# Decode attention beside a gated feed-forward block: key and value tiles of two heads interleaved over partitions, keys transposed as 32-bit pairs

## The chip, the cores and the metric

The kernel runs on one core of a Trainium2 chip. The time is that of the device in microseconds; a kernel is run several times, and only runs in the fast state are compared, by a ratio to runs of the kernel before in the same rounds. A run more than 1.5% above the fastest of its kernel counts as slow; the text says where that was so. A difference is called settled at 2% only where the whole 95% interval of the ratio lies beyond 2%. A profile is one execution. Engines are named as the profile does: PE is TensorE (PEld its weight loads), DVE is VectorE, ACT is ScalarE, SP issues the loads. Each engine has its own list of instructions, its queue. Semaphores tie the lists together.

## The reference

Only the attention part matters here. Four sequences decode one token each. There are 32 query heads over 8 key/value heads, of width 128, and the last 4096 positions of the cache are used:

```python
q = (x @ wq)                                   # 4 x 32 heads x 128
k = k_cache[:, :, Sk - 4096:, :]               # 4 x 8 heads x 4096 x 128, bf16: 33.5 MB
v = v_cache[:, :, Sk - 4096:, :]               # the same again
p = softmax(q @ k.T * 128 ** -0.5)
a = (p @ v) @ wo                               # wq, wo: 4.2 MB each
b = relu(x @ W_gate) * (x @ W_up) @ W_down     # 1.8 MB each
out = g * a + (1 - g) * b                      # g: a sigmoid gate per sequence
```

In all 81 MB are read, and next to nothing is written. Each key is used by four queries only, so the work per byte is small, but keys arrive with the position on the partitions, and both kernels transpose them on the chip so that the score product can contract over the head width.

## The kernel before

32 heads are handled in 8 sets of four. A key tile is one head: 128 partitions with 32 positions each, so that a partition reads one run of 8 KB.

```python
# loads, all from SP
e.dma_start(Ksb[:, slot, :], A_k_cache[bb, kvh, SK-WIN:SK, :].rearrange("(p c) d -> p (c d)", p=128))

def _act_copies_kt(g, i):                      # which key evictions ScalarE makes
    j = g % 4
    return (j, i) in ((2, 1), (2, 3), (3, 1), (3, 3))

# TensorE's order (cut): KT key transposes, PV value product, PT probability transposes, SC scores
for s in range(NSET + 2):
    for j in range(4):
        g = 4 * s + j
        for i in range(4): order.append(("KT", g, i))
        if s >= 2 and j == 1: order.append(("PV", s - 2, 0, 16))
        if s >= 2 and j == 2: order.append(("PV", s - 2, 16, 32))
    for i in range(4): order.append(("PT", s - 1, i))
    for i in range(8): order.append(("SC", s, i))
```

A fill is one PSUM bank. KT fills a bank with eight 128x128 bf16 transposes, and DVE or ACT copies ("evicts") it to SBUF; there are four such banks, so a fill waits for the eviction of the fill four before it. SC makes scores of 4 heads in four column groups of PE; DVE evicts them and takes the maximum; ACT makes the exponentials in four pieces of 1024 columns. PV is made of 128 small matmuls per set, in four column groups. The weights wo come last of all loads.

## Time and profile before

| | before |
|---|---|
| time | 210.8 us (210.76 to 210.85) |
| span of the profile | 209.4 us |
| load stream | about 419 GB/s, no gap |
| time from one set's exponentials to the next's, sets 2 to 7 | 19.0 us |
| last load lands (landing records of the trace) | 201.1 us |

These lines of the page are the busy time and share of each engine, the mean busy share of the 16 DMA engines in 40 slices of the span (9 is 90% or more), what they moved, and the load queue's packets, megabytes and share of 16 engines' span.

```profile
PE 146.9 (70%) x3007; PEld 119.3 (57%) x3007; DVE 128.4 (61%) x338; ACT 86.4 (41%) x116; POOL 0.7 (0%) x6
...
DMA  4999999999999999999999999999999999999710
GB/s 131 415 424 426 412 403 436 412 423 418 423 421 413 419 419 419 423 419 421 423 416 412 423 415 419 419 426 419 415 415 418 421 423 421 415 419 419 299 42 1
...
q1 hardware_dynamic: 12136, 81.02, 93.7%
```

The DMA row is full from slice 2 to 37. The kernel is bound by its loads, and every engine has slack on average.

### The profile page before, as it was taken

The numbers are of one execution on the slowest core, as the hardware profiler recorded it, in microseconds if no ns is written. First come the engines' busy times: TensorE is split into PE (matmuls) and PEld (weight loads), VectorE is DVE, ScalarE is ACT, GpSimd is POOL, SyncE is SP. The second block draws the span as 40 slices with busy tenths as digits, with TensorE's granted clock in tenths as the row PEclk, the third lists the DMA queues.
The fourth block names the chain that finished last, engine by engine and source line by source line (L and its number), as shares of the span: only waits on it lengthen the run. The fifth ranks groups of instructions, "written<-read, shape, count | busy, mean of one in ns | idle before, by whom it ended". The sixth has DMA issues, their size and how long they took to land.

```text
span 209.4 us, 6715 instructions
## 1 busy us (share of the span) xinstructions
PE 146.9 (70%) x3007; PEld 119.3 (57%) x3007; DVE 128.4 (61%) x338; ACT 86.4 (41%) x116; POOL 0.7 (0%) x6
## 2 busy tenths in 40 slices
PE   0029917659997869797797777876976797756362
PEld 0028915459993758486396736753873677345251
DVE  4002914952459927994996499769948975942121
ACT  2000123280271836195466428551754565193000
POOL 1000000000000000000000000000000000000000
PEclk9999988968599997999969999999999999985555
DMA  4999999999999999999999999999999999999710
GB/s 131 415 424 426 412 403 436 412 423 418 423 421 413 419 419 419 423 419 421 423 416 412 423 415 419 419 426 419 415 415 418 421 423 421 415 419 419 299 42 1
DMA packets 12164, 81.43 MB, mean 389 GB/s; under 512 B 1764, under 2 KB 1768, under 8 KB 2792
## 3 DMA queue, kind: packets, MB, share of 16 engines
q1 hardware_dynamic: 12136, 81.02, 93.7%
q8 instruction: 23, 0.38, 0.7%
q14 instruction: 5, 0.04, 0.0%
HBM read 81.01 MB, written 0.00 MB: 387 GB/s over the span
## 4 chain that ended last, share of the span: by engine, by line
PE 44%; DMA 19%; DVE 16%; SPq 10%; issue 9%; DVEq 0%
PE bank L556 23%; DVE sc L765 11%; DMA Ksb<-in_A_k_cache_dram 10%; DMA Vsb<-in_A_v_cache_dram 9%; PE bank L625 8%; SPq L462 7%; PE bank L594 5%; PE bank L524 3%; PE bank L654 2%; DVE X L800 2%; DVE Ksb L752 2%; PE bank L582 2%; SPq L449 1%; SPq L445 1%; SPq L451 1%
## 5 line engine op out<-in xcount | busy, mean ns | idle before, releaser
L556 PE MATMUL bank<-ident,Ksb 128*128 128x128 bf16 x1024 | 74.5, 236 | 17.1 <-DMA Ksb<-in_A_k_cache_dram 9.2
L556 PEld LDWEIGHTS bank<-ident,Ksb 128*128 128x128 bf16 x1024 | 66.6, 107 | 23.6 <-DMA Ksb<-in_A_k_cache_dram 9.7
L752 DVE COPY Ksb<-bank 128x1024 bf16<-128x1024 bf16 x96 | 61.0, 684 | 30.9 <-PE bank L556 30.7
L872 ACT ACTIVATE Ksb<-bank 128x1024 bf16<-128x1024 bf16 x32 | 31.6, 1022 | 47.2 <-PE bank L556 47.2
L881 ACT ACTIVATE sc<-sc,negmax 128x1024 bf16<-128x1024 bf16 x32 | 36.3, 1137 | 33.3 <-DVE negmax L776 33.3
L765 DVE TENSOR_SCALAR_CACHE_REDUCE sc<-bank 128x512 bf16<-128x512 f32 x64 | 39.8, 687 | 2.4 <-PE bank L582 1.7
L582 PE MATMUL bank<-Ksb,qT 128*4 128x512 bf16 x256 | 22.5, 378 | 11.5 <-DVE sc L765 9.7
L625 PE MATMUL bank<-Vsb,pT 128*4 128x128 bf16 x1024 | 19.2, 230 | 10.2 <-issue 8.2
L625 PEld LDWEIGHTS bank<-Vsb,pT 128*4 128x4 bf16 x1024 | 15.8, 89 | 12.6 <-issue 11.2
L582 PEld LDWEIGHTS bank<-Ksb,qT 128*4 128x4 bf16 x256 | 5.4, 81 | 27.0 <-DVE sc L765 22.7
L594 PE MATMUL bank<-ident,sc 128*128 128x128 bf16 x256 | 17.2, 225 | 2.2 <-ACT sc L881 2.1
L594 PEld LDWEIGHTS bank<-ident,sc 128*128 128x128 bf16 x256 | 15.5, 101 | 3.1 <-ACT sc L881 3.0
L872 ACT ACTIVATE pT<-bank 128x1024 bf16<-128x1024 bf16 x16 | 15.6, 1026 | 0.3 <-PE bank L594 0.2
L752 DVE COPY pT<-bank 128x1024 bf16<-128x1024 bf16 x16 | 11.0, 690 | 6.5 <-PE bank L594 6.5
L800 DVE COPY X<-bank 32x16 bf16<-32x16 bf16 x32 | 6.0, 186 | 9.0 <-PE bank L635 8.7
L497 PE MATMUL bank<-xT,Wbig 128*128 128x4 bf16 x128 | 3.6, 166 | 11.1 <-DMA Wbig<-in_A_wq_dram 11.1
L497 PEld LDWEIGHTS bank<-xT,Wbig 128*128 128x128 bf16 x128 | 3.5, 104 | 11.2 <-DMA Wbig<-in_A_wq_dram 11.2
L706 DVE CAST qT<-bank 128x128 bf16<-128x128 f32 x1 | 0.3, 292 | 14.5 <-PE bank L497 14.5
L855 ACT ACTIVATE gsb<-bank 1x4 f32<-1x4 f32 x1 | 0.2, 163 | 16.9 <-PE bank L505 16.9
L524 PE MATMUL bank<-xT,Vsb 128*128 128x4 bf16 x112 | 6.8, 199 | 0.0
L524 PEld LDWEIGHTS bank<-xT,Vsb 128*128 128x128 bf16 x112 | 6.8, 161 | 0.0
L881 ACT ACTIVATION_READ_ACCUMULATOR sc<-sc,negmax 128x1 f32 x32 | 6.0, 186 | 0.0
(44 smaller groups left out, 36.6 us busy)
## 6 DMA issues: line engine op xcount, KB each, us to landing
Ksb<-in_A_k_cache_dram SPq DMA_DIRECT2D x32, 1024.0 KB, 18.7
Vsb<-in_A_v_cache_dram SPq DMA_DIRECT2D x32, 1024.0 KB, 19.0
Wbig<-in_A_wq_dram SPq DMA_DIRECT2D x4, 1024.0 KB, 8.4
Wbig<-in_A_wo_dram SPq DMA_DIRECT2D x4, 1024.0 KB, 22.8
Vsb<-in_B_W_gate_dram SPq DMA_DIRECT2D x1, 1792.0 KB, 22.4
Vsb<-in_B_W_up_dram SPq DMA_DIRECT2D x1, 1792.0 KB, 24.8
Vsb<-in_B_W_down_dram SPq DMA_DIRECT2D x1, 1792.0 KB, 21.4
out_dram<-out SPq DMA_DIRECT2D x4, 1.0 KB
```

The lines of the kernel that those rows point to most:

```text
L462: E.op(lambda bb=bb, kvh=kvh, slot=slot: e.dma_start(Ksb[:, slot, :], A_k_cache[bb, kvh, SK - WIN:SK, :].rearrange("(p c) d -> p (c d)", p ...
L497: E.op(lambda H=H, tt=tt: t.matmul(qb[:, Q_COL + H * 4:Q_COL + (H + 1) * 4], Wbig[:, tt, H * 128:(H + 1) * 128], xT[:, tt * 4:(tt + 1) * 4 ...
L524: E.op(lambda W=W, col0=col0, i=i, tt=tt: t.matmul(gub[:, col0:col0 + 4], W[:, tt, i:i + NFT * 127 + 1:NFT], xT[:, tt * 4:(tt + 1) * 4], s ...
L556: E.op(lambda bk=bk, cc=cc, ch=ch, k3=k3: t.transpose(bankbf[bk][:, cc * 128:(cc + 1) * 128], k3[:, ch, :], ident[:, :]), produces=[(f"trf ...
L582: E.op(lambda bk=bk, j=j, lhsT=lhsT, rhs=rhs: t.matmul(banks[bk][32 * j:32 * j + 4, 0:512], lhsT, rhs, start=True, stop=True, tile_positio ...
L594: E.op(lambda bk=bk, cc=cc, ch=ch, par=par: t.transpose(bankbf[bk][:, cc * 128:(cc + 1) * 128], sc[:, par, ch * 128:(ch + 1) * 128], ident ...
L625: E.op(lambda ob=ob, j=j, par=par, ch=ch, v3=v3: t.matmul(ob[32 * j:32 * j + 4, 0:128], pT[:, par, ch * 128 + 32 * j: ch * 128 + 32 * j + ...
L752: E.op(lambda dst=dst, bk=bk: v.tensor_copy(dst, bankbf[bk][:, :]), produces=[copy_ctr(key)], waits=w)
L765: E.op(lambda par=par, i=i, bk=bk: v.tensor_scalar(sc[:, par, i * 512:(i + 1) * 512], banks[bk][:, :], 1.0, None, op0=ALU.mult, op1=ALU.ma ...
L800: E.op(lambda dst=dst, srcv=srcv: v.tensor_copy(dst, srcv), produces=[("dtrc", copy_event(key))] if q == 3 else [], waits=[("TRF",) + key] ...
L872: E.op(lambda dst=dst, bk=bk: a.activation(dst, bankbf[bk][:, :], ACTF.Copy), produces=[copy_ctr(key)], waits=w)
L881: E.op(lambda par=par, piece=piece: a.activation(sc[:, par, piece * n:(piece + 1) * n], sc[:, par, piece * n:(piece + 1) * n], ACTF.Exp, b ...
```

## The change

It is a rewrite with these parts. A tile is two heads, with even partitions for one and odd for the other, so that a partition reads 16 KB. Two neighbouring bf16 elements are transposed as one 32-bit word, so that half as many transposes are needed; even and odd elements of the head then lie side by side, and the score product is made in two passes over every second element, with a query matrix that has zeros where the other position's words lie. wo is loaded early, and half of its product is made before the end; the last value tile comes in quarters; many small steps at the end are gone. Its intent is faster loads and a shorter tail.

```diff
-                    Ksb[:, slot, :], A_k_cache[bb, kvh, SK - WIN:SK, :].rearrange("(p c) d -> p (c d)", p=128)),
+                     A_k_cache[b, h:h + 2, SK - WIN:SK, :].rearrange("h (r c) d -> r h (c d)", r=64), waits=w)
...
-    return (j, i) in ((2, 1), (2, 3), (3, 1), (3, 3))
+    return f in ((3, 7) if i % 2 == 0 else (1, 4, 7))
...
+    for s in range(2, NSET):
+        o += [("KT", 2 * s), ("PT", s - 1), ("PV", s - 2), ("RS", s - 2), ("KT", 2 * s + 1), ("OQ", s - 2), ("SC", s), ("SW", s)]
+        if s == 6:
+            o.append(("WO", 0))
...
+                        rhs = kt2((2 * s + pair) % KSLOTS)[:, 8 * f:8 * f + 8, jp:128:2, e]
+                        mm(bk[32 * j:32 * j + 8, :], qblk[:, g, 8 * e:8 * e + 8], rhs, e == 0, e == 1, ...)
...
+            mm(banks[OB][32 * pair:32 * pair + 8, 0:128], pT[:, s % 2, c0:c0 + 8],
+               Vsb[:, (2 * s + pair) % VSLOTS, 128 * ch:128 * ch + 128], ch == 0, ch == 63, pos=(0, 32 * pair))
...
+                E.op(lambda r=r, n=n: a.activation(pev[r, :, n], sc[r, :], ACTF.Exp, ...)   # pev: every second element
```

(All cuts are marked with "..."; the rest of the diff replaces helpers, the small projections and the end.) KT now has two tiles of eight fills per set; RS, SW and OQ are small matmuls for the sums, the maximum and the output layout.

## The prediction

> **What bounds the kernel now.** The load stream. In the page's 40 slices the DMA row is 9 from slice 2 to slice 37 and moves about 419 GB/s; section 3 gives the load queue 93.7% of 16 engines' span. Every compute engine has slack: PE is 70% busy, DVE 61%, ACT 41%. The period of a set of four heads is 19.9 us (timeline, score matmuls at 100.8 and 120.6 us), which is its 8.4 MB at 420 GB/s. SP's own waits show that loads are issued far ahead (19 us from issue to landing), so short compute stalls do not reach the stream. The last data land at about 197.7 us, and 11.7 us of tail follow: two output transposes with slow strided copies (0.8 us per set), 128 small WO matmuls at half clock (3.7 us), combine, transpose, four stores. Only the stream and this tail are on the critical path.
>
> **Stream.** Packet records: a 3584 B packet takes 142 ns, 8192 B 312 ns (mean 315), 14336 B 540 ns. That is a line of 0.037 ns per byte plus about 8 ns. The skill's "DMA: Bandwidth & Descriptors", section "Why small descriptors are slow", has a fixed cost per packet of the same kind. Estimate for 16 KB: 616 to 622 ns, against 2 x 315. K and V (67 MB) save 2 to 3.7 us, the gate and up loads (3.5 KB runs become 14 KB) 0.6, wq 0.3; WO (4 KB runs) and the quartered last V lose 0.2. The 512 two-byte packets of gate_w, which now do not precede the large loads, save about 0.4. Sum: 3 to 4.5 us. The last byte lands at about 193.7 us.
>
> **Tail.** WO is loaded early, and half of its product is done before the end. After the last quarter of V: 16 PV matmuls (1 to 1.7 us), normalise 0.5, 16 tiny selection matmuls and a copy 1.5, 8 WO matmuls of 512 columns (1.7 warm, 3.4 at half clock, plus 0.3 latency), one combine 0.7, one store and end 2.7. Estimate 9.3 us in place of 11.7. Gain about 2.4.
>
> **Off the path.** Score columns per set and number of score matmuls are unchanged, but the evictions fall from 8 to 4 per set (0.69 us each); K copies stay at 128 (0.68 DVE, 1.02 ACT); PT copies halve; DVE falls to about 12.5 us per set. PV packs two column groups instead of four: from 2 to about 4 us per set. K transposes fall from 1024 bf16 to 512 of 32 bits. If each costs what a bf16 one does (60 ns), PE needs some 12 us per set; at 270 ns it needs 25, and the kernel becomes PE-bound. "TensorE: Matmul & The Clock Gate", Terms, says that transpose mode is four times faster for FP32; no run here shows it yet. I expect 60 to 130 ns.
>
> **Prediction.** Span 203 us, measured time 204.4 us (the measured time lies 1.4 over the span); 8 in 10: 201 to 209. Faster by over 2%: 0.72; within 2%: 0.19; slower: 0.09.
>
> **What would show it.** DMA slices at 425 to 428 GB/s; 16 KB packets of 616 to 622 ns; last V landing near 193.7; 9 to 9.5 us from there to the end; SP never the cause of a DMA gap; K transposes under 130 ns apiece; PE at half clock or better in the tail.
>
> **What would make it wrong.** 32-bit transposes slow enough (over about 190 ns) that PE paces each set; alternating between two heads 4 MB apart slowing HBM reads, so that 16 KB packets take 640 ns or more; the 8-byte-strided score operand streaming at half rate; PE instruction stalls or a cold clock in the tail; or a longer start, as K0 goes ahead of wq.

## More of the kernel before

The timeline of the kernel before, PE alone (start, duration, engine, line, operation, output<-inputs, shapes, count, and in brackets the idle time before it with what ended it), through one set:

```profile
104.80 5.67 PE L556 MATMUL bank<-ident,Ksb 128*128 128x128 bf16 x64
110.40 1.06 PE L625 MATMUL bank<-Vsb,pT 128*4 128x128 bf16 x64
111.40 1.96 PE L556 MATMUL bank<-ident,Ksb 128*128 128x128 bf16 x32
...
118.72 2.00 PE L594 MATMUL bank<-ident,sc 128*128 128x128 bf16 x32
```

PE goes from keys to values to keys without waiting for ACT, and comes to the probability transposes (118.72) long after the exponentials that they need.

The end of the timeline: the value product of the last set begins when the last values land, the product with wo (which lands until 201.1) follows, then the store:

```profile
191.43 3.58 PE L625 MATMUL bank<-Vsb,pT 128*4 128x128 bf16 x127 [1.94 <-DMA Vsb<-in_A_v_cache_dram]
...
201.45 3.35 PE L654 MATMUL bank<-oq,Wbig 128*128 128x4 bf16 x120 [0.41 <-DVE oq L732]
...
206.81 1.30 SPq L472 DMA_DIRECT2D out_dram<-out  x4
```

```profile
106.61 1.15 ACT L881 ACTIVATE sc<-sc,negmax 128x1024 bf16<-128x1024 bf16 x1 [4.69 <-DVE negmax L776]
...
110.02 1.13 ACT L881 ACTIVATE sc<-sc,negmax 128x1024 bf16<-128x1024 bf16 x1
...
112.50 1.94 ACT L872 ACTIVATE Ksb<-bank 128x1024 bf16<-128x1024 bf16 x2 [1.26 <-PE bank L556]
```

The fourth exponential ends at 111.2 us, and ACT's next duty, a key eviction, does not begin before 112.50 and had to wait for PE. Nobody waits for the exponentials.

## The result

| | before | changed |
|---|---|---|
| time, median | 210.8 us | 238.5 us (237.54 to 239.63) |
| ratio of the fast runs | | 1.131, 95% interval 1.128 to 1.135 |
| span of the profile | 209.4 us | 237.9 us |
| PE busy, 100 to 160 us of the span | 47.6 us | 47.2 us |
| last load lands | 201.1 us | 211.1 us |

A ratio here is the mean time of one kernel's fast runs over that of the other's of the same rounds, so it is not quite the ratio of the medians. The change is 13% slower; a gain of 3% had been predicted.

The same lines of the page, changed kernel, with the row of the granted PE clock (in tenths of full speed):

```profile
PE 176.6 (74%) x2346; PEld 127.7 (54%) x2346; DVE 109.5 (46%) x249; ACT 86.2 (36%) x78; POOL 2.9 (1%) x15
...
PEclk9995967979998599979985999799959999999599
DMA  5999999999999999999999959995899990630000
GB/s 220 414 427 420 437 425 429 427 438 422 393 418 433 435 419 422 435 430 419 424 424 426 419 220 391 435 416 191 372 435 430 422 424 22 222 134 3 0 3 1
...
q1 hardware_dynamic: 6816, 81.01, 81.4%
```

The packets are little more than half as many, and while the stream runs it does run at 425 GB/s. But from the middle on it has holes, and after slice 33 it breaks down. The compute side hands back buffers too late: in the timeline below SP issues the next key load at 141.41 us, just after the last scores that read the buffer (141.36), and slice 24 (136.8 to 142.7 us) moves 220 GB/s. This happens although no engine is near full: PE is at 74% against 70%, and DVE is at 46% against 61% and ACT at 36% against 41%.

When the first exponential of each set starts (timelines of ACT) shows where the time goes:

| set | 0 | 1 | 2 | 3 | 4 | 5 | 6 | 7 | end of span |
|---|---|---|---|---|---|---|---|---|---|
| before, us | 41.8 | 68.4 | 88.7 | 106.6 | 126.5 | 145.5 | 164.5 | 183.7 | 209.4 |
| changed, us | 42.6 | 71.0 | 95.1 | 118.8 | 143.0 | 166.6 | 190.8 | 212.8 | 237.9 |
| later by | 0.8 | 2.5 | 6.4 | 12.2 | 16.5 | 21.1 | 26.3 | 29.2 | 28.5 |

The start and the time after the last exponentials (25.7 and 25.1 us) are nearly equal. The loss arises in the sets, mostly 4 to 6 us in each. From set 2 to set 6 a set takes 23.9 us (95.7 over 4), while the stream needs 19.7 for its 8.4 MB (estimate: 8.4 MB at 425 GB/s).

The timeline of the changed kernel through one such set, exponentials to exponentials, ACT, PE and one load issue of SP (SPq):

```profile
118.82 2.62 ACT L689 ACTIVATE pe<-sc,negmax 64x2048 bf16<-64x2048 bf16 x1 [5.63 <-DVE negmax L602]
...
121.51 2.56 ACT L689 ACTIVATE pe<-sc,negmax 64x2048 bf16<-64x2048 bf16 x1
...
124.14 1.02 ACT L666 ACTIVATE Ksb<-bank 128x1024 bf16<-128x1024 bf16 x1
...
125.22 1.11 PE L328 MATMUL bank<-identf,Ksb 128*128 128x128 f32 x4 [3.69 <-ACT Ksb L666]
...
126.12 1.06 PE L324 MATMUL bank<-sel,pe 128*128 128x32 bf16 x32
...
127.11 5.30 PE L324 MATMUL bank<-Vsb,pT 128*8 128x128 bf16 x128
...
132.55 3.74 PE L328 MATMUL bank<-identf,Ksb 128*128 128x128 f32 x32
...
136.32 1.02 ACT L666 ACTIVATE Ksb<-bank 128x1024 bf16<-128x1024 bf16 x1 [0.31 <-PE bank L328]
...
137.49 3.87 PE L324 MATMUL bank<-Ksb,qblk 128*8 128x512 bf16 x32 [0.95 <-ACT Ksb L666]
...
141.41 0.54 SPq L250 DMA_DIRECT2D Ksb<-in_A_k_cache_dram  x1
...
142.96 2.63 ACT L689 ACTIVATE pe<-sc,negmax 64x2048 bf16<-64x2048 bf16 x1 [5.61 <-DVE negmax L602]
```

This is a loop with no slack in it. The exponentials take until 124.1. Behind them *in ACT's queue* is one key eviction (124.14). PE stands still for 3.69 us before its last key fill, because the bank it needs is that eviction's. Behind the fill *in PE's queue* are the probability transposes (126.12), the value product (127.11, 5.3 us), and the second key tile (132.55). ACT evicts its last fill (136.32); the scores wait 0.95 us for that and take 3.87; the maximum follows, and then the next exponentials. PE works for some 18 us of the 24 and waits in order for the rest. In the kernel before, neither queue had such an obstacle.

The costliest groups of the changed kernel that lie on this loop (line, engine, operation, names, shapes, count | busy us, mean ns of one | idle time just before them and what ended most of it):

```profile
L328 PE MATMUL bank<-identf,Ksb 128*128 128x128 f32 x512 | 68.0, 292 | 36.2 <-ACT Ksb L666 22.1
...
L689 ACT ACTIVATE pe<-sc,negmax 64x2048 bf16<-64x2048 bf16 x16 | 41.5, 2592 | 46.8 <-DVE negmax L602 46.6
L324 PE MATMUL bank<-Vsb,pT 128*8 128x128 bf16 x1024 | 44.3, 253 | 0.6 <-DVE recip L612 0.6
...
L324 PE MATMUL bank<-Ksb,qblk 128*8 128x512 bf16 x256 | 31.6, 624 | 6.9 <-ACT Ksb L666 6.9
```

The mean duration of a pipelined matmul is not its rate. The rates come from the timeline: a 32-bit transpose 117 ns (32 in 3.74 us), a value matmul 41 ns in this set (128 in 5.30 us), and 29 ns where the clock was full (128 in 3.74 us, at 198.6 us).

The stretches around that stand-still (from : to, length, busy time of each engine, then granted PE clock, DMA share, GB/s):

```profile
core 0: us, PE busy (x) PEld busy (x) DVE busy (x) ACT busy (x) POOL busy (x), PEclk, DMA share, GB/s
...
121.60:125.20 3.60, 0.00 (x0) 0.00 (x0) 1.01 (x2) 3.54 (x3) 0.00 (x0) 0.78 1.01 432
125.20:127.10 1.90, 1.88 (x36) 1.80 (x36) 0.31 (x1) 0.73 (x1) 0.00 (x0) 0.50 1.03 440
...
131.00:132.50 1.50, 1.50 (x54) 1.39 (x46) 0.00 (x0) 0.00 (x0) 0.00 (x0) 1.00 0.90 371
```

While PE idles from 121.6 to 125.2 its granted clock falls. It is 0.50 during the probability transposes and half of the value product, and full again by 131. The Trainium skill, "TensorE: Matmul & The Clock Gate", Part 1, describes this: after an idle window of about 3.4 us the clock is halved until PE has been busy for about as long. The trace agrees in kind: the profile counts six such waits of up to 3.7 us, and the records of the clock show a stretch of 3.4 or 6.8 us at 0.5 that begins within 1.7 us of the end of each of the six, before it in four and after it in two. How short a wait can be and still have this effect is a question to which experiments 1 and 11 return. So the wait is paid for twice (experiment 9 tests this).

The end of the changed kernel (timeline): the last exponential, the value product of the last set's first tile, the last eight matmuls of the output projection, and the combine.

```profile
215.50 2.56 ACT L689 ACTIVATE pe<-sc,negmax 64x2048 bf16<-64x2048 bf16 x1
...
220.21 6.47 PE L324 MATMUL bank<-Vsb,pT 128*8 128x128 bf16 x64 [0.56 <-DVE recip L612]
...
233.53 1.89 PE L324 MATMUL bank<-Wbig,oq 128*4 128x512 bf16 x8 [0.32 <-DVE oq L636]
235.46 0.74 DVE L652 SCALAR_TENSOR_TENSOR osum<-bank,gg,t 4x512 bf16<-4x512 f32 x1 [1.98 <-PE bank L324]
```

The end does not follow the last byte either: from 211.1, where that lands, it is still 26.8 us. The end is the chain behind the last scores.

### The profile page after: what moved, and what is told of

Same layout as the page of the kernel before. It is cut to its first block, busy times and chain, and to the rows that moved or that the text cites. A ratio compares the mean times of both kernels' runs of the same rounds, so it can differ in the third digit from the quotient of the medians.

```text
span 237.9 us, 5144 instructions
## 1 busy us (share of the span) xinstructions
PE 176.6 (74%) x2346; PEld 127.7 (54%) x2346; DVE 109.5 (46%) x249; ACT 86.2 (36%) x78; POOL 2.9 (1%) x15
## 4 chain that ended last, share of the span: by engine, by line
PE 57%; ACT 24%; DVE 8%; DMA 7%; issue 2%; SPq 1%; ACTq 0%; DVEq 0%
PE bank L324 41%; ACT pe L689 18%; PE bank L328 16%; DMA Wbig<-in_A_wq_dram 7%; ACT Ksb L666 6%; DVE sc L591 2%; DVE pe L581 1%; DVE qblk L573 1%; SPq L250 1%; DVE rowmax L595 1%; DVE hmax L600 1%; DVE negmax L602 1%; DVE pT L607 1%; DVE osum L652 0%; DVE osb L616 0%
## 5 line engine op out<-in xcount | busy, mean ns | idle before, releaser
L328 PE MATMUL bank<-identf,Ksb 128*128 128x128 f32 x512 | 68.0, 292 | 36.2 <-ACT Ksb L666 22.1
L328 PEld LDWEIGHTS bank<-identf,Ksb 128*128 128x128 f32 x512 | 60.8, 151 | 39.5 <-ACT Ksb L666 23.9
L666 ACT ACTIVATE Ksb<-bank 128x1024 bf16<-128x1024 bf16 x40 | 41.0, 1024 | 75.0 <-PE bank L328 74.8
L689 ACT ACTIVATE pe<-sc,negmax 64x2048 bf16<-64x2048 bf16 x16 | 41.5, 2592 | 46.8 <-DVE negmax L602 46.6
L324 PE MATMUL bank<-Vsb,pT 128*8 128x128 bf16 x1024 | 44.3, 253 | 0.6 <-DVE recip L612 0.6
L324 PEld LDWEIGHTS bank<-Vsb,pT 128*8 128x8 bf16 x1024 | 42.7, 102 | 0.8 <-issue 0.6
L324 PE MATMUL bank<-Ksb,qblk 128*8 128x512 bf16 x256 | 31.6, 624 | 6.9 <-ACT Ksb L666 6.9
L591 DVE TENSOR_SCALAR_CACHE_REDUCE sc<-bank 128x512 bf16<-128x512 f32 x32 | 22.1, 692 | 18.9 <-PE bank L324 18.9
L607 DVE CAST pT<-bank 128x512 bf16<-128x512 f32 x16 | 10.3, 685 | 21.9 <-PE bank L324 21.8
L324 PE MATMUL bank<-sel,pe 128*128 128x32 bf16 x256 | 8.0, 181 | 1.9 <-ACT pe L689 1.9
```

The lines of the kernel that those rows point to most:

```text
L324: E.op(lambda: t.matmul(out_, lhsT, rhs, start=start, stop=stop, tile_position=pos, skip_group_check=True), ev=ev, waits=waits)
L328: E.op(lambda: t.transpose(out_, in_, idn), ev=ev, waits=waits)
L591: E.op(lambda: v.tensor_scalar(sc[:, 512 * f:512 * f + 512], banks[scb(key)], 1.0, None, op0=ALU.mult, op1=ALU.max, accum_out=mx4[:, f:f + ...
L607: E.op(lambda: v.tensor_copy(pT[:, s % 2, 512 * f:512 * f + 512], banks[tr(key)]), ev=("E",) + key, waits=[key] + ([("PV", s - 2)] if s >= ...
L666: E.op(lambda: a.activation(kt_dst(i, f), bankb[tr(key)], ACTF.Copy), ev=("E",) + key, waits=[key])
L689: E.op(lambda r=r, n=n: a.activation(pev[r, :, n], sc[r, :], ACTF.Exp, bias=negmax[r, s % 2:s % 2 + 1], scale=SCALE, accum_out=rowsum[r, s ...
```

## The experiments

The theory at the start, A: the loop through two in-order queues paces the sets. The rival, B: PE's own work does (slower transposes, value product in two column groups), and order is immaterial. Twelve kernels were run; all give the reference's result except where noted. Times are medians of all runs of a kernel, and the ratio, of fast runs alone, is that to the kernel before.

### 1. Evictions out of the way of the exponentials

```diff
-    return f in ((3, 7) if i % 2 == 0 else (1, 4, 7))
+    return i % 2 == 1 and f % 2 == 1          # ACT evicts for the second tile of a set only
```

> Edit: the key evictions of even tiles all go to VectorE, odd tiles keep four on ScalarE; nothing else. Theory A (a loop through in-order queues: the exponentials of set s-1 sit in ScalarE's queue ahead of the key evictions of set s, and the probability transposes sit in TensorE's queue ahead of the value product): TensorE no longer waits for a ScalarE eviction after the exponentials, but still waits for the exponentials themselves at the probability transposes. The set period falls by about 1.7 us (one eviction of 1.0 and its fill of 0.65), from 23.9 to about 22.2 us, the time to 226 to 230 us. Theory B (TensorE's own work, slower 32-bit transposes and two-group value products, paces a set and order is immaterial): 237 to 240 us, no change.

Measured: 224.9 us (ratio 1.068, 1.061 to 1.076), a period of 22.3 us over sets 1 to 7 in place of 23.6. Theory A holds, B does not; the gain is a little larger than expected, and the time 1 us below the range. PE still waits 2.1 us for the exponentials, now at the probability transposes:

```profile
116.20 1.01 PE L324 MATMUL bank<-sel,pe 128*128 128x32 bf16 x32 [2.14 <-ACT pe L689]
```

The clock records of this run show a stretch at 0.5 that begins within 1.7 us of the end of such a wait in three of five sets, so even this shorter wait can lower the clock.

### 2. Probability transposes later

```diff
-  ("KT", 2*s), ("PT", s-1), ("PV", s-2), ("RS", s-2), ("KT", 2*s+1), ...
+  ("KT", 2*s), ("PV", s-2), ("RS", s-2), ("KT", 2*s+1), ("PT", s-1), ...
```

> Edit: in TensorE's order the probability transposes of set s-1 move from after the first key tile of set s to after its second; evictions as in the changed kernel. Theory A: TensorE still stops at the eighth fill of the first key tile, whose bank waits for a ScalarE eviction queued behind the exponentials, so the wait is the same and the time stays at 235 to 240 us. Theory B: no change either.

Measured: two fast runs of 230.3 and 232.9 us (ratio 1.101, 1.090 to 1.112) and two over 234 that count as slow. In the profile, which is one of the slow ones (236.7 us), a set takes 23.8 us over sets 2 to 6, as good as unchanged, PE waits 3.69 us six times as before, and this is what A expected. B expected no change either, so this run alone does not tell them apart. The gain of 6 to 8 us in the fast runs was not expected, and as none of these was profiled, its place is open. The four runs line up with their mean granted clock (230.3 us at 0.918, 232.9 at 0.904, 234.2 at 0.897, 236.7 at 0.884), but the clock is not all of it: two runs of the changed kernel at 0.906 took 237.5 and 237.9 us.

### 3. Both

> Both edits. Theory A: the exponentials leave the loop (5.3 us of ScalarE now run beside the value product and the second key tile); what is left is TensorE's own work, about 20 to 20.5 us per set; 211 to 218 us. Far more than the sum of the two edits alone. Theory B: 237 to 240 us.

Measured: 216.4 us (ratio 1.027, 1.018 to 1.036; three fast runs of 215.1 to 217.6, and one of 219.6 that counts as slow). It is inside the expected range, and still slower than the kernel before, though whether by 2% is not settled; but it was not "far more than the sum": 22 us against 14 and about 7. The gain stopped at a floor. The page and ACT's timeline of this kernel:

```profile
DMA  5999999999999999999999999999999999994000
GB/s 221 412 448 390 426 430 439 422 425 427 434 391 410 437 427 433 421 424 430 427 424 427 427 417 436 427 424 411 436 427 417 427 439 424 417 401 180 3 3 1
```

```profile
111.14 2.59 ACT L689 ACTIVATE pe<-sc,negmax 64x2048 bf16<-64x2048 bf16 x1
...
118.00 3.77 ACT L666 ACTIVATE Ksb<-bank 128x1024 bf16<-128x1024 bf16 x4 [4.22 <-PE bank L328]
```

The stream has no hole up to its end, and the last load lands at 196.7 us, 4.4 us before that of the kernel before. The eviction that followed the exponentials at once now comes 4.2 us after them, and ACT waits for PE. With some evictions moved from ACT to DVE and one step of PE moved in its order, and no change in what any operation computes, the sets are bound by the loads again: 19.3 us each from set 2 to set 6. So PE's own work, with its 32-bit transposes and two-group value product, fits.

### 4. Both, and the value product in four column groups

```diff
-            mm(banks[OB][32 * pair:32 * pair + 8, 0:128], ..., ch == 0, ch == 63, pos=(0, 32 * pair))
+            r0 = 32 * pair + 64 * (ch % 2)    # even and odd chunks apart, summed by the one-hot matmul OQ
+            mm(banks[OB][r0:r0 + 8, 0:128], ..., ch < 2, ch > 61, pos=(0, r0))
```

> Both edits, and the value product over four column groups (even and odd chunks in different groups, summed by the selection matmul), so that it costs about 2.0 us a set in place of 5.3. Theory A: TensorE's work per set falls to about 17 us, below the 19.7 us that the loads of a set take; the load stream is saturated again to the end and the time is 201 to 207 us, below the kernel before. Theory B: a gain of 3.3 us in each of 8 sets, to about 212 us, and no more.

Measured: 216.6 us (ratio 1.029, 1.023 to 1.035): no gain over experiment 3, and the expectation of 201 to 207 missed. The value product did fall to 1.96 us per set. But the stream was the limit already, and the end is not the stream. PE's timeline at the end of this kernel:

```profile
180.85 4.95 PE L330 MATMUL bank<-identf,Ksb 128*128 128x128 f32 x32 [3.71 <-issue]
...
186.98 3.85 PE L326 MATMUL bank<-Ksb,qblk 128*8 128x512 bf16 x32
...
197.76 1.03 PE L326 MATMUL bank<-sel,pe 128*128 128x32 bf16 x32 [3.55 <-ACT pe L693]
...
199.84 3.58 PE L326 MATMUL bank<-Vsb,pT 128*8 128x128 bf16 x64 [0.38 <-DVE recip L614]
...
209.47 1.89 PE L326 MATMUL bank<-Wbig,oq 128*4 128x512 bf16 x8 [0.32 <-DVE oq L640]
```

The last keys landed at 177.1 us and the last values at 196.7. From the keys to the end it is 36.7 us: a stall of 3.7 us that is put down to no engine ("issue"; a 16 KB instruction packet moved at 178.3 us, so it is probably the fetch of instructions, which no run settles), transposes at a lowered clock, scores, 5.3 us of exponentials before any probability can be transposed, two value products one after the other, the projection. The values need 19.6 us to land after the keys, so the chain is longer. This is theory C: **the last keys set the end, not the last byte.** Its rival D: it is the work after the last byte.

### 5. wo after the last keys

```diff
-        if i == 4:
+        if i == NPAIR - 1:
             o.append(("wo",))
```

(and the first half of its product moves to the end). 

> Base: the kernel with both order edits and four-group value products (216.6 us), whose stream was saturated to 196.7 us and which still ended at 213.8. One edit: the 4.2 MB output projection weights are loaded after the last key tile and not among the early loads, so that the last keys land 10 us earlier while the last byte of V still lands last, at the same time. Theory C (the end is a chain of 36 us from the landing of the last keys: transposes, scores, exponentials in two halves, value products, projection): the chain moves forward up to 10 us and the end is then set by the last V: 205 to 210 us. Rival D (the end is set by the work after the last byte of V, which is merely longer than estimated): no change, 215 to 218 us.

Measured: 211.9 us (ratio 1.010, 1.001 to 1.020: within 2% of the kernel before). With the same last byte (196.6 us) the end came 4.7 us earlier; D is out. It missed the range by 2 us: the last keys landed at 166.7 and the last exponentials began at 178.8 in place of 192.4, but the next thing in PE's queue is the value product of set 6. Its second value tile now lands at 186.7, behind wo, and PE stood still for 8.45 us in front of it. Again one queue, in order.

### 6. wo last of all, as in the kernel before

The four value tiles come right after the last keys, then wo in four pieces, and its product is made at the very end. 

> Same base; the output projection weights are now the very last load, in four pieces, as in the kernel before, and the projection is computed at the end, 1.9 us of it after the last piece. Theory C: keys and values land 10 us earlier, attention is done by the time the last piece of weights lands at 196.7 us, and only 8 matmuls, the combine and the store follow: 202 to 206 us. Rival D: the value product no longer follows the last byte, so also a gain; this run is for the size of what the early load of these weights cost, and for a kernel faster than the one before (210.7 us).

Measured: 206.25 us (ratio 0.980, 0.973 to 0.988), a quarter of a microsecond above the range. This kernel is faster than the one before, as the whole interval lies under 1; whether by 2% is not settled. Loading wo early, one of the intents of the change, had delayed all later keys by 10 us and so the end of the chain.

### 7. Only the four-group value product, on the changed kernel

> Base: the changed kernel as it is (238.5 us). One edit: the value product over four column groups. In the loop of theory A every piece of TensorE work counts while the loop is longer than the loads of a set: the product falls from 5.3 to 2.0 us, the period from 23.9 to about 20.6 us, the time to 212 to 220 us. If the two-group product were hidden (not on the loop), no change: 236 to 240 us.

Measured: 228.2 us (ratio 1.085, 1.076 to 1.095). The product is on the loop, so it gains 10 us; but that misses the expected 212 to 220, since at 120 us of its profile it took 3.58 and not 1.96 us: it runs right after the stand-still of 3.69 us, at half clock.

### 8. Contiguous operands

```diff
-  rhs = kt2(slot)[:, 8 * f:8 * f + 8, jp:128:2, e]        # every fourth element
+  rhs = Ksb[:, slot, 2048 * f + 1024 * jp + 512 * e:... + 512]
-  a.activation(pev[r, :, n], ...)                          # every second element
+  a.activation(pe[r, 2048 * n:2048 * n + 2048], ...)
```

> Wrong result on purpose. Base: the changed kernel. Two access patterns are made contiguous with the same number of elements: the moving operand of the score matmuls (was every fourth 2-byte element) and the output of the exponentials (was every second). If the 8-byte stride halves the streaming rate, eight score matmuls take about 0.45 us in place of 0.9, VectorE's eviction (0.70) paces them and the scores of a set take about 3.2 us in place of 3.9; if it does not matter, 3.9 stays. If the strided output slows the exponentials, an instruction takes about 2.0 us in place of 2.59; if not, 2.59 stays. Theory A: both lie on the loop, so the set period falls by about 1.9 us, to about 22 us, and the time to 222 to 229 us.

Measured, one run, of which the state is unknown: 215.1 us, result wrong as intended. The same groups as shown above for the changed kernel:

```profile
L689 ACT ACTIVATE pe<-sc,negmax 64x2048 bf16<-64x2048 bf16 x16 | 32.0, 2000 | 38.2 <-DVE negmax L602 38.0
...
L324 PE MATMUL bank<-Ksb,qblk 128*8 128x512 bf16 x256 | 20.1, 408 | 9.7 <-ACT Ksb L666 6.9
```

An exponential takes 2.00 us in place of 2.59; the mean score matmul takes 408 ns in place of 624. In the timeline of the changed kernel the weight loads of four score matmuls, which run side by side, start 0.46 us apart (137.46, 137.92, 138.39); with contiguous operands the groups of four start 0.21 us apart (122.85, 123.07, 123.28, 123.50 in the records of this trace). So both strides cost; experiments 11 and 12 test whether each cost lay on the loop. The gain of 23 us exceeds the expected 9 to 16. The stand-still fell to 2.5 us and the clock dropped after fewer of them, which goes with this; its share was not measured. The row of DMA is that of experiment 3, digit for digit: with shorter pieces on the loop the same order lets the stream run full to its end at 196.6 us. It takes the order and the length of the pieces together to make the loop too long.

### 9. Useless work in the stand-still

```diff
+  if f == 7 and i % 2 == 0 and i >= 2:      # before the last fill of a set's first key tile
+      for r in range(14): mm(bank of the scores already evicted, qblk[:, 0, 0:8], qblk as 512 columns, True, True)
```

> Base: the changed kernel as it is (238.5 us). One edit: 14 score-sized matmuls whose result nobody reads are put into TensorE's queue just before the last fill of each first key tile, where TensorE stands still for 3.7 us per set behind ScalarE; they last about 3.0 us and take nothing away. Theory: the stand-still does not only cost its own 3.7 us, it also lowers the granted clock to 0.5 for the 3.4 to 6.8 us after it, which is where the value product runs; with the filler the clock stays at 1.0, the product takes 3.7 us in place of about 5.3, the period falls by 1.5 to 1.7 us and the time to 225 to 230 us, although TensorE does more work. Rival (the two-group product takes 5.3 us at any clock): no gain, 238 to 241 us.

Measured: 233.2 us (ratio 1.113, 1.104 to 1.122). The filler and what follows, PE's timeline:

```profile
117.11 3.19 PE L324 MATMUL bank<-qblk 128*8 128x512 bf16 x14
...
120.88 0.66 PE L328 MATMUL bank<-identf,Ksb 128*128 128x128 f32 x4 [0.59 <-ACT Ksb L671]
...
122.26 3.46 PE L324 MATMUL bank<-Vsb,pT 128*8 128x128 bf16 x118
```

The wait shrinks to 0.59 us (the bank comes free no earlier), the page's row of the granted clock shows 9 from slice 8 to slice 37, and 118 value matmuls take 3.46 us, 29 ns each. The kernel does more work and is 5 us faster: so the falling clock has a cost of its own, and 5 us is what the filler won back of it, net. The rival is out, but it is less than the 8 to 13 us expected. Most traced sets lasted 22.1 us in place of 23.9, but one 23.6 (in it, 1.4 us of "issue" in the middle of the value product), and the last one 25.1. In the changed kernel that last one took 22.1 already: half of the output projection, 2.75 us of real matmuls, stands in the queue just there, the wait was 0.31 us and the value product took 3.74 us. Real work had the filler's effect, and the filler on top of it only cost its own 3 us.

### 10. The last value tile in one piece, on the kernel of experiment 6

> Base: the kernel with both order edits, four-group value products and the output weights loaded last (206.25 us; last byte at 198.2 us). One edit: the last value tile is loaded in one piece (16 KB packets) and not in four (4 KB packets); it is no longer the last load, so the pieces buy nothing. A 4 KB packet took 160 to 172 ns, four of them 640 to 690 against 611 to 622 for one of 16 KB, on 32 large packets per engine: 0.8 to 2 us of stream. Theory: the last byte lands 0.8 to 2 us earlier, 204.0 to 205.8 us. Rival: the end is set by the work after the value product, no change, 206 to 207 us.

Measured: 205.2 us (ratio 0.979, 0.972 to 0.985: faster than the kernel before, whether by 2% not settled; five fast runs and one of 209.6 that counts as slow). The last load lands at 197.8 in place of 198.2 us. So the time lies in the expected range, but by luck: 0.4 us earlier had been put at 0.8 to 2. The expectation counted 32 large packets per engine; the tile is 128 of them over 16 engines, 8 each, which at the same packet times makes 0.1 to 0.6 us (estimate). The intervals of 6 and 10 overlap and they ran on different chips, so whether the piece size helps is not settled. It is the fastest kernel. Its page:

```profile
DMA  5999999999999999999999999999999999999940
GB/s 201 428 408 427 424 421 433 435 422 436 431 419 424 434 427 418 427 431 414 427 434 418 431 431 424 418 434 421 421 427 424 431 424 421 427 428 397 405 169 1
```

Full from slice 2 to 38, at 425 GB/s, and then 4.7 us from the last landing to the end of its span (202.5), where the kernel before needed 8.3 (209.4 less 201.1).

### 11. Contiguous exponentials only

> Wrong result on purpose. Base: the changed kernel as it is (238.5 us). One edit: the exponentials write their 2048 elements side by side and not to every second place (an instruction then takes 2.0 us in place of 2.59, as the run with both dense accesses showed). Theory: two of them stand between TensorE and its last fill, so its stand-still falls from 3.7 to about 2.5 us, [...]so that the value product runs at full clock too (3.7 to 4.6 us in place of 5.3): 2 to 2.8 us per set, 217 to 224 us. Rival (the length of the stand-still has nothing to do with the clock): only 1.2 us per set, 228 to 231 us.

Measured: 225.8 us (ratio 1.071, 1.068 to 1.074), result wrong. It lies between the two expectations. The stand-still fell to 2.60 us; the clock still dropped after some of them (value product 5.37 us at 119.6) and not after others (3.74 us at 142.2; no stretch at half clock from 123 us to the last exponentials). So the shorter stand-still saves the clock in some sets only.

### 12. Contiguous scores only

> Wrong result on purpose. Base: the changed kernel as it is. One edit: the score matmuls read 512 neighbouring elements and not every fourth. Theory: the scores of a set shorten by about 1.2 us, all of it on the loop, and the stand-still of 3.7 us with its halved clock stays: 1.2 us in each of 8 sets, 226 to 231 us. Rival (the scores are hidden behind VectorE's evictions): no change, 237 to 240 us.

Measured: 227.7 us (ratio 1.078, 1.072 to 1.084), inside the range. The scores are not the right ones; the comparison with the reference let them pass all the same, which says that it is not sensitive to the scores of this input. The gains of 11 and 12 (12.7 and 10.8 us) add up to that of 8 (23.4).

## Why the prediction was wrong

**Right, where nothing holds it up: the stream.** A 16 KB packet was put at 616 to 622 ns; the median is 611 in the changed kernel and 613 in experiment 3, just below. In experiment 3 the last load lands 4.4 us before that of the kernel before; 3 to 4.5 had been predicted. The absolute 193.7 was off, since the last landing before was read as 197.7 from the throughput row, while the landing records show 201.1: the 16 landings of the last load are spread from 195.9 to 201.1 us, and the last one counts. No cost of alternating between two heads 4 MB apart shows.

**Right as a size, wrong as a worry: the transposes.** They take 117 ns, inside 60 to 130, and per set as long as twice the number of bf16 ones did (64 x 117 against 128 x 61 ns, from 32 in 1.96 us).

**Wrong: "Every compute engine has slack" and "short compute stalls do not reach the stream".** This is the step that failed. Both were read from the kernel before and carried over to a program with a different order. The busy shares of the changed kernel are as low as before; they show nothing of a loop that goes through several engines one at a time. The prediction added up the work of PE and DVE per set, which fits into 19.7 us (experiment 3 shows it), and never followed one set through the queues: exponentials, eviction behind them, fill, probability transposes, values, keys, scores, exponentials, 23.9 us. So compute stalls did reach the stream: it broke off, and the last load landed at 211.1 us in place of 193.7. The order of both queues was in the diff.

**Wrong: terms left out or too small.** The exponentials were not costed at all: 2 x 2.59 us, of which 2 x 0.6 is the strided output. The scores were counted as unchanged: their stride costs 1.2 us per set (named among the risks, without a size). The value product was put at 4 us and took 3.7 at full clock and up to 5.4 after a stand-still. PE was put at some 12 us per set with transposes of 60 ns; in the set shown it is busy for 18.5 of 24.1 us, part of it at half clock. The falling clock was named for the tail only; it acts in six of the eight sets.

**Wrong: the tail.** It was costed as what follows the last byte, 9.3 us. In experiment 4, with a full stream, it is the chain of 36.7 us that follows the last *keys*. Loading wo early lets the keys land late. A short tail does exist once the keys are early enough, 4.7 us in experiment 10, but it is that behind wo loaded last, not the predicted one behind the last values.

**What each repair is worth** does not add up over all five, although two pairs that were tested did (1 and 2 in 3; 11 and 12 in 8). On the changed kernel alone: evictions 13.6 us, order of the probability transposes about 7, four column groups 10.3, contiguous exponentials 12.7, contiguous scores 10.8. Their sum is twice the loss of 27.7 us, and they cannot all be had: they shorten the same loop, and experiment 4 shows that the gain stops where the stream takes over.

## What to carry to other kernels

Busy shares bound a pipeline from below only; for a new order, follow one iteration through every in-order queue, add up what stands behind what, and compare that loop with the period of the stream. Do not put an eviction that the matmuls need behind a long activation in the same queue, and do not put the consumer of that activation ahead of independent matmuls. When loads bound a kernel, look for the load with the longest chain behind it, which set the end here: bring that one early, and leave for the end the one with the least left to do.

## What the Trainium skill lacked or had wrong

- "SBUF — State Buffer", Specifications (TRN2), asks for at least two hits per 16-byte line for full bandwidth. The scores' operand has two 2-byte elements in each such line (8 bytes apart), and yet it streamed at less than half rate: 0.46 us from one group of four concurrent matmuls of 512 columns to the next, against 0.21 when contiguous (experiment 8). So two hits were not enough here; the measurement decides.
- "ScalarE: Activation LUTs", section "What ACT_TABLE_LOAD costs", gives about 1990 ns for 2048 columns with a bias operand. The contiguous exponentials agree (2.00 us); it says nothing of strided output, where 2-byte elements at every second place took 2.59 us.
- "TensorE: Matmul & The Clock Gate", Part 1, speaks of idle windows of about 3.4 us. A stand-still of 2.60 us was enough for half clock in some sets here and not in others (experiment 11), and so was one of 2.14 us (experiment 1). In the kernel before the clock also fell, for 3.4 us at 104.9, though in the 6 us before that PE waited no longer than 0.4 us at a time (between score matmuls). What decides it is open.
- No page gives the rate of 32-bit transposes: Part 4 of "TensorE: Matmul & The Clock Gate" times bf16 ones alone, and its Terms have only the factor that the prediction quotes. Here it is 117 ns against 61 for bf16.
